# A two-convolution residual block with row transforms: a second PSUM bank for the outer products, the outer sums moved to the end, an opening on TensorE, and a searched assignment of engines

## Chip, cores, metric

One core of one Trainium2 chip. The metric is the device time of one execution in microseconds (us); a kernel's time is the median of its runs. The run of 569.85 us of the kernel before is 1.6% above that kernel's fastest, so it counts as slow and is left out of the ratio below (it is still in the median of 564.35 us; without it the median is 563.33). The profiled span is about 2 us shorter than the time.

## The reference

```python
B, C, HW, E = 2, 512, 64, 1152            # bf16 inputs
def gn(z, gamma, beta): ...               # 4 groups of 128 channels, mean and variance over group and image
def conv3(z, w): ...                      # 3x3, padding 1, 512 -> 512 channels
h = conv3(silu(gn(x, g1, be1)), w1)
h = h + (silu(t_emb) @ w_emb).reshape(B, C, 1, 1)
h = conv3(silu(gn(h, g2, be2)), w2)
return x + h
```

## The kernel before

The 3x3 convolution is computed with transforms over the rows: four output rows come from six products. Planes 0 to 3 ("inner") are sums and differences of input rows, planes 4 and 5 ("outer") serve only the first and the last of the four output rows. VectorE makes the planes ("row sums"), TensorE (PE) multiplies, ScalarE takes the products out of PSUM, and VectorE adds them up to rows. The inner products of chunks 1 to 7 are transformed once more over the columns, which gives B and A matmuls of 256 columns; the others have 512.

The work is cut in 8 chunks (layer, image, half) of four *units* (128 output channels each). Chunks 0 to 3 are layer 1. While the units of chunk c are multiplied, VectorE makes the planes of chunk c+1. The counts of convolution matmuls are 288 in chunk 0, 320 in each of chunks 1 to 3 and 352 in each of 4 to 7, 2656 in all.

The kernel records every operation with its reads and writes and an assumed duration. When the program is built, a list scheduler in the kernel decides the order of each engine's operations. A different assumed duration, or one changed operation, can thus reorder everything.

The end of a unit of layer 2, with cuts marked:

```python
def evac_o(s, bank):                     # outer product -> OO[s - 4], by ScalarE
    act(A(OO[s - 4], [[1, 512]]), Ps(bank, 0, [[1, 512]]), ...)
# ... in unit(c, k), layer 2; `next_pair` cycles through banks 0-1, 2-3, 4-5:
run([(6, 4, plain_mms)]);  evac_o(4, 6)
run([(p1, 0, B_mms), (p1 + 1, 2, B_mms)]);  evac_b(0, p1)
run([(6, 5, plain_mms)]);  evac_o(5, 6)                   # bank 6 again
# ... B of planes 1 and 3, s_ops: BT -> SD
run([(p3, 0, A_mms), (p3 + 1, 2, A_mms)]);  evac_pair(0, p3)     # -> M0, M2
run([(p4, 1, A_mms), (p4 + 1, 3, A_mms)]);  evac_pair(1, p4)     # -> M1, M3
TT(M(0, 4), M(0, 4), A(SD, [[512, 4], [1, 512]]), ALU.add)
TT(two(SD, 512), M(0, 2), M(2, 2), ALU.add)               # s
TT(M(0, 2), M(0, 2), M(2, 2), ALU.subtract)               # d
scal(..., M(2), M(1), -8.0); scal(..., M(3), M(1), -2.0)  # engines by SENG[l]
scal(..., A(SD + 1024, ...), A(SD + 512, ...), 4.0)
tt(M2 and S1, M2 and S1, two(OO[1], OO[0] - OO[1]), ALU.add)     # the outer sum
tt(yr(0),  MB broadcast, M2 and M3, ALU.add)              # rows 0, 1 of the output
tt(yr(16), SD broadcast, S2 and S1, ALU.add)              # rows 2, 3
```

`MB` (M0 to M3), `SD` (S0 to S2) and `BT` exist once. ScalarE may write them for the next unit only when VectorE has read them for this one. Nearly all buffers are stretches of one SBUF array, `ar`.

The small matmuls of the group statistics (`gn_chain`) write two columns of bank 7. The first layer's weights are prepared in chunk 0 by `prep_w1`: a load, two scalings by ScalarE, three or four sums by VectorE.

Of the kernel before, what the change touches and what calls it, by code (L numbers as in the profile page):

```python
# [21 lines left out]
class Op:  # L22
    __slots__ = ("i", "eng", "cost", "lat", "fn", "preds", "succs", "name", "pri", "start", "hold")


class Plan:
# [3 lines left out]
    ENG = ("PE", "DVE", "ACT", "POOL", "DMA", "SW")  # L30
    LAT = {"PE": 0.12, "DVE": 0.1, "ACT": 0.15, "POOL": 0.15, "DMA": 2.0, "SW": 2.6}
# [14 lines left out]
    def op(self, eng, cost, fn, r=(), w=(), name="", chain=False, lat=None, after=()):  # L46
# [3 lines left out]
        o.hold = 0.0  # L50
        deps = set(after)
# [33 lines left out]
    def edge_lat(self, a, b):  # L85
        if a.eng == b.eng:
            return a.lat if a.eng in ("DMA", "SW", "DVE", "POOL") else (0.0 if a.eng == "PE" else a.lat)
        return a.lat

    def _run(self, pri, back):  # L90
# [11 lines left out]
        while done < n:  # L102
# [6 lines left out]
            win = bt + 0.03  # L109
# [76 lines left out]
KAP = (1.0 / 6.0, 1.0 / 24.0, 1.0 / 6.0, 1.0 / 24.0)  # L186

SZ = {}
# [3 lines left out]
def kernel(  # L192
# [15 lines left out]
    UREG, UM = [], 10240  # L208
# [3 lines left out]
    VB = [o, o + 16512 + 14496]  # L212
    Z = o + 16512
    o += 33024 + 14496
    AB = [o, o + AF]
    o += 2 * AF
    WB = o
    o += KF + 1
# [8 lines left out]
    W2O = [Z + 3840, Z + 5376]  # L227
    X0 = Z + 6912
# [3 lines left out]
    O0 = [Z + 11552, Z + 12576]  # L232
# [9 lines left out]
    NF = 480  # L242
# [93 lines left out]
    def dma(out, in_, r, w, nbytes, name="", sw=False, acc=False):  # L336
        rate = 0.14 if (sw and acc) else 0.28
        kw = {"accum_op": ALU.add, "max_dma_last_dim": 2080} if acc else {}
        eng = nc.gpsimd if sw else nc.sync
        pl.op("DMA" if not sw else "SW", nbytes / rate * 1e-6 if nbytes > 30000 else 0.1,  # L340
              lambda: eng.dma_start(out=out, in_=in_, **kw), regs(*r), regs(*w), name)  # L341
# [5 lines left out]
    def mm(lst, name="", chain=True):  # L347
        rr, ww, cost = [], [], 0.0
        for out, lhsT, rhs, st, sp in lst:
            rr += [lhsT, rhs]  # L350
            ww.append(out)
            cost += max(0.06, rhs.n / 2290.0)

        def fn():
            for out, lhsT, rhs, st, sp in lst:
                nc.tensor.matmul(out.ap, lhsT=lhsT.ap, rhs=rhs.ap, start=st, stop=sp, skip_group_check=True)  # L356
        pl.op("PE", cost, fn, regs(*rr), regs(*ww), name, chain=chain)
# [14 lines left out]
    WARM = Fc(2)  # L372
    NEGH = Fc(1)
# [23 lines left out]
    SB = 7  # L397

    def gn_chain(layer, b, ct, mes, name):
# [6 lines left out]
        mm(lst, name, chain=False)  # L406
# [37 lines left out]
    def row_w(w0, w2z, mid, o_um, name):  # L444
# [9 lines left out]
        tt(A(o_um, [[384, 2], [512, 3], [1, 128]]), p3, m, ALU.add, name)  # L454
        tt(A(o_um + 256, [[-128, 2], [512, 3], [1, 128]]), p3, m, ALU.subtract, name)
# [67 lines left out]
    def mode(c):  # L523
        return "N" if c == 0 else ("0" if c < 4 else "1")
# [19 lines left out]
    def load_a(c, ct, resident=None):  # L544
        l, b, ch = chunks[c]
        ab = AB[acnt[0] % 2]
        acnt[0] += 1
        acur[(c, ct)] = (ab, resident)
        nm = f"a{c}{ct}"
        if resident is not None:  # L550
            return
# [15 lines left out]
    def silu(c, ct):  # L567
        l, b, ch = chunks[c]
        ab, res = acur[(c, ct)]
        r0 = RW if ch == 0 else 0  # L570
        dims = [[RW, 33], [33, 2], [1, 32]]
        src = ab if res is None else res
        act(A(ab + r0, dims), A(src + r0, dims, BF16 if l == 0 else None), ACT.Silu,
            scale=F(scol(l, b, ct)), bias=F(ncol(l, b, ct)), name=f"silu{c}{ct}")

    def rows(c, ct, keng="ACT", seng="DVE"):
        ab, _ = acur[(c, ct)]
        nm = f"row{c}{ct}"
        scal(keng, A(WB, [[1, KF]]), A(ab, [[1, KF]]), 4.0, f"k{c}{ct}")
        S, D = ALU.subtract, ALU.add  # L580
        two = lambda base, r0, r1: A(base + r0 * RW, [[(r1 - r0) * RW, 2], [1, PL]])
        tt(two(WB, 9, 17), two(WB, 9, 17), two(ab, 1, 26), S, nm)
        tt(two(WB, 0, 25), two(WB, 0, 25), two(ab, 9, 17), S, nm)
        s4, s5 = vplane(c, ct, 4), vplane(c, ct, 5)
        tt(A(s4, [[s5 - s4, 2], [1, PL]]), two(WB, 0, 25), two(WB, 9, 17), S, nm)
        tt(two(WB, 0, 17), two(ab, 1, 25), two(ab, 9, 17), S, nm)
        t2b = A(WB + 17 * RW, [[1, PL]])
        scal(seng, t2b, t2b, 2.0, nm)
        Q, SS = two(WB, 9, 0), two(WB, 25, 17)
# [7 lines left out]
        for k, op in ((0, D), (2, S)):  # L597
            tt(A(o[k], [[o[k + 1] - o[k], 2], [1, PL]]), Q, SS, op, nm)
        if md == "N":
            return  # L600
# [3 lines left out]
        for kind, (i, j, op) in enumerate(((32, 33, S), (1, 0, S), (33, 0, S), (33, 0, D))):  # L604
# [48 lines left out]
    def unit(c, k, order=None, banks=None):  # L653
# [7 lines left out]
        if md == "1":  # L661
            BT, SD = BT1, SD1
            OO = [UREG[2 * (u % 2)] + 9728, UREG[2 * (u % 2) + 1] + 9728]
        else:
            BT, SD = BT0, SD0
            OO = [O0[u % 2], O0[u % 2] + 512]
        if l == 0 and ch == 0:
            SSUM[(b, k)] = (Fc(12), Fc(2))
        acc = lambda i: None
        if l == 0:  # L670
            cs, cq = SSUM[(b, k)]
            acc = lambda i: F(cs + 6 * ch + i)

        def evac_o(s, bank):
            act(A(OO[s - 4], [[1, 512]]), Ps(bank, 0, [[1, 512]]), ACT.Identity if l == 0 else ACT.Copy,
                scale=(0.25, 1.0)[s - 4], acc=acc(s), name=nm + f"o{s}")

        def evac_m(s, bank, i):
            act(M(s), Ps(bank, 0, [[1, 512]]), ACT.Identity if l == 0 else ACT.Copy, scale=KAP[s], acc=i, name=nm + f"m{s}")
# [4 lines left out]
        def evac_b(s, bank):  # L684
            i = (s // 2) if md == "0" else s
# [7 lines left out]
        def run(steps):  # L693
            for bank, s, fn in steps:
                for ct in range(CT):
                    mm(fn(bank, c, k, ct, s), nm + f"{fn.__name__[0]}{s}")

        TT = tt
        nf = {"N": 0, "0": 2, "1": 4}[md]

        def s_ops():
            g = lambda q: A(BT + q * 256, [[512, nf], [32, 8], [1, 32]])
            TT(A(SD, [[512, nf], [64, 8], [1, 32]]), g(0), g(1), ALU.add, nm + "S")
            TT(A(SD + 32, [[512, nf], [64, 8], [1, 32]]), g(0), g(1), ALU.subtract, nm + "S")

        if order == "ct":
            return
        if md == "N":
            p1, p2 = (banks or (next_pair(), next_pair()))
            run([(6, 4, plain_mms)])  # L710
            evac_o(4, 6)
            run([(p1, 0, plain_mms), (p1 + 1, 2, plain_mms)])
            evac_m(0, p1, acc(1))
            evac_m(2, p1 + 1, None)
            run([(6, 5, plain_mms)])
            evac_o(5, 6)
            run([(p2, 1, plain_mms), (p2 + 1, 3, plain_mms)])
            evac_m(1, p2, acc(3))
            evac_m(3, p2 + 1, acc(2))
        elif md == "0":  # L720
# [3 lines left out]
            run([(p1, 0, B_mms), (p1 + 1, 2, B_mms)])  # L724
            evac_b(0, p1)
            s_ops()
            run([(6, 5, plain_mms)])
            evac_o(5, 6)
            run([(p2, 0, A_mms), (p2 + 1, 2, A_mms)])
            evac_m(0, p2, acc(1))  # L730
            evac_m(2, p2 + 1, None)
            TT(M(0, 2, 1024), M(0, 2, 1024), A(SD, [[512, 2], [1, 512]]), ALU.add, nm + "A")
# [3 lines left out]
        else:  # L736
# [5 lines left out]
            run([(6, 5, plain_mms)])  # L742
            evac_o(5, 6)
# [7 lines left out]
            TT(M(0, 4), M(0, 4), A(SD, [[512, 4], [1, 512]]), ALU.add, nm + "A")  # L751

        two = lambda off, st: A(off, [[st, 2], [1, 512]])
        TT(two(SD, 512), M(0, 2), M(2, 2), ALU.add, nm + "s")
        TT(M(0, 2), M(0, 2), M(2, 2), ALU.subtract, nm + "d")
        se = SENG[l]
        scal(se[0], M(2), M(1), -8.0, nm + "8")
        scal(se[1], M(3), M(1), -2.0, nm + "2")
        scal(se[2], A(SD + 1024, [[1, 512]]), A(SD + 512, [[1, 512]]), 4.0, nm + "4")

        tt(two(MB + 1024, SD + 512 - MB - 1024), two(MB + 1024, SD + 512 - MB - 1024), two(OO[1], OO[0] - OO[1]),
           ALU.add, nm + "O")
        yr = lambda r0: A(ys + r0 * RW, [[RW, 16], [33, 2], [1, 32]])
        tt(yr(0), A(MB, [[0, 2], [64, 8], [1, 64]]) if False else A(MB, [[0, 2], [1, 512]]),
           A(MB + 1024, [[512, 2], [1, 512]]), ALU.add, nm + "y")
        tt(yr(16), A(SD, [[0, 2], [1, 512]]), A(SD + 1024, [[-512, 2], [1, 512]]), ALU.add, nm + "y")
        yv = A(ys, [[1, YF]])
        if l == 0:
            dma(h_scr[b, k, ch], yv.ap, [yv], [K("h", b, k, ch)], P * YF * 2, nm + "st")
            act(A8(JNK, YF), yv, ACT.Square, scale=float(HW) ** -0.5, acc=F(cq + ch), name=nm + "sq")  # L770
            if ch == 1:
                gn2(b, k)
        else:
            dma(out[b, k, ch], yv.ap, [yv, K("o", b, k, ch)], [K("o", b, k, ch)], P * YF * 2, nm + "out", sw=True, acc=True)
        ucnt[0] += 1

    SENG = {0: ("DVE", "DVE", "DVE"), 1: ("ACT", "ACT", "ACT")}

    def gn2(b, k):
        cs, cq = SSUM[(b, k)]  # L780
        m0, me, wj, ws = Fc(2), Fc(2), Fc(12), Fc(1)
# [32 lines left out]
    def stats0(ct):  # L814
# [3 lines left out]
        x0 = A(XB0[ct] + RW, [[1, YF]], BF16)  # L818
        x1 = A(XB1[ct], [[1, YF]], BF16)
        bk = 4 + (ct % 2)  # L820
        lst = []
        for h, base in enumerate((XB0[ct] + RW, XB1[ct])):
            for i in range(5):
                lst.append((Ps(bk, 0, [[1, 416]]), cone, A(base + i * 416, [[1, 416]], BF16),
                            h == 0 and i == 0, h == 1 and i == 4))
        mm(lst, nm, chain=False)
        junk = A(MB + (ct % 2) * 512, [[1, 416]], BF16)
        act(junk, Ps(bk, 0, [[1, 416]]), ACT.Identity, scale=1.0 / (P * HW), acc=F(me), name=nm)
        act(A8(JNK, YF), x0, ACT.Square, scale=float(HW) ** -0.5, acc=F(me + 1), name=nm)
        bg = ct % 4  # L830
        lst = []
        for i in range(17):
# [178 lines left out]
```

## Time and profile before

| | before |
|---|---|
| time, median (lowest to highest) | 564.35 us (560.69 to 569.85), 4 runs |
| profiled span, mean granted clock | 558.7 us, 0.943 |
| matmuls of 512 / 256 columns | 1248 / 1408 |
| VectorE: 16-bit sums of 1024 elements | 304, 0.692 us each as recorded |

From the page of the kernel before: the busy times with their shares of the span, and busy tenths in 40 slices with the clock that PE was granted.

```profile
## 1 busy us (share of the span) xinstructions
PE 479.6 (86%) x2853; PEld 280.0 (50%) x2853; DVE 446.8 (80%) x943; ACT 404.7 (72%) x627; POOL 36.7 (7%) x62
...
PE   5649996999798889898997789987999896989990
...
DVE  1898898896599897987677999898899888974543
ACT  6998787699798968584565878565889776655551
...
PEclk9959997999999989999997879998999997999995
```

No engine is busy all the time. From its waits (who waited for whom, total us, times, longest):

```profile
ACT ar L328 <- PE psum L356: 72.3, 67, 5.5
DVE ar L305 <- ACT ar L328: 55.3, 45, 2.9
ACT ar L328 <- DVE ar L305: 46.0, 35, 5.4
...
PE psum L356 <- DVE ar L305: 38.1, 16, 5.4
PE psum L356 <- ACT ar L328: 15.0, 7, 4.9
```

ScalarE waits for PE, VectorE for ScalarE, ScalarE for VectorE, and PE for both: a ring. L328 is the line of all ScalarE operations, L305 of all VectorE sums, L356 of all matmuls. Four stretches of PE's timeline (start, length, what; in brackets the idle time before it and what ended it):

```profile
30.74 1.44 PE L356 MATMUL psum<-ar 128*128 128x512 f16 x3 [5.09 <-DVE ar L305]
37.58 43.96 PE L356 MATMUL psum<-ar 128*128 128x512 f16 x186 [5.40 <-DVE ar L305]
...
204.18 30.43 PE L356 MATMUL psum<-ar 128*128 128x512 f16 x160 [2.45 <-ACT ar L328]
...
469.39 30.30 PE L356 MATMUL psum<-ar 128*128 128x512 f16 x188 [4.89 <-ACT ar L328]
```

The first two are the opening, which waits for row sums. The other two are the first matmul of the second outer block, which waits for bank 6. Three windows of layer 2 (length, then busy us and count of PE, weight loads, VectorE, ScalarE, POOL; clock; DMA share; GB/s):

```profile
380.00:400.00 20.00, 18.79 (x118) 12.02 (x117) 17.11 (x42) 15.45 (x19) 3.57 (x4) 0.93 0.51 100
400.00:420.00 20.00, 18.84 (x146) 14.17 (x146) 19.57 (x43) 15.92 (x15) 4.14 (x5) 1.00 0.66 159
420.00:440.00 20.00, 17.31 (x119) 11.28 (x118) 18.09 (x34) 15.77 (x16) 1.46 (x4) 1.00 0.46 119
```

### The profile page before, as it was taken

Reading aid. Unit: us, or ns where it says so; the run is one execution under the profiler, and the core shown is the slowest. Engines: PE = TensorE matmul, PEld = TensorE weight load, DVE = VectorE, ACT = ScalarE, POOL = GpSimd, SP = SyncE. Lnnn points to the kernel's source line nnn. Section 1 sums busy time; section 2 is a strip of 40 time slices with the busy share of each in tenths; the row PEclk is TensorE's granted clock in tenths of the full one; section 3 lists DMA queues with packets and bytes.
Section 4 is the critical chain, followed back from the end, with each engine's and each line's share of the span. In section 5 each row is a group of like instructions: output and inputs, shape, how many; then the busy total and the mean of one; then the engine's idle time right before and its main releaser. Section 6 shows DMA issues by size and latency. Waiting matters only on the chain.

```text
span 558.7 us, 8160 instructions
## 1 busy us (share of the span) xinstructions
PE 479.6 (86%) x2853; PEld 280.0 (50%) x2853; DVE 446.8 (80%) x943; ACT 404.7 (72%) x627; POOL 36.7 (7%) x62
## 2 busy tenths in 40 slices
PE   5649996999798889898997789987999896989990
PEld 3414442455354445454553356655666563767760
DVE  1898898896599897987677999898899888974543
ACT  6998787699798968584565878565889776655551
POOL 2100000000000000000000000101210000001000
PEclk9959997999999989999997879998999997999995
DMA  8576556766645345333445543564556564454432
GB/s 338 213 226 211 158 164 189 240 230 193 223 166 181 127 131 193 125 134 114 175 175 182 181 144 101 136 160 104 118 153 136 135 152 88 98 121 93 65 54 38
DMA packets 37465, 86.11 MB, mean 154 GB/s; under 512 B 6064, under 2 KB 15792, under 8 KB 37424
## 3 DMA queue, kind: packets, MB, share of 16 engines
q1 hardware_dynamic: 32784, 77.06, 42.3%
q0 software_dynamic: 4352, 8.52, 10.4%
q8 instruction: 22, 0.36, 0.3%
q14 instruction: 19, 0.16, 0.1%
q10 hardware_dynamic: 288, 0.01, 0.0%
HBM read 62.25 MB, written 31.85 MB: 168 GB/s over the span
## 4 chain that ended last, share of the span: by engine, by line
issue 19%; DVE 15%; PE 10%; ACT 5%; DMA 3%; POOL 2%; POOLq 0%; DVEq 0%; SPq 0%; ACTq 0%
DVE ar L305 14%; PE psum L356 10%; ACT ar L328 5%; DMA ar<-h_scr 2%; POOL out_dram L341 2%; DMA ar<-in_w_dram 1%; DVE ar L309 0%; POOL fs L415 0%; POOLq L1006 0%; DVEq L305 0%; DVE fs L801 0%; DVE fs L422 0%; DVE fs L409 0%; DVE fs L420 0%; DVE fs L408 0%
## 5 line engine op out<-in xcount | busy, mean ns | idle before, releaser
L356 PE MATMUL psum<-ar 128*128 128x512 f16 (+2 forms) x2732 | 462.0, 330 | 51.6 <-DVE ar L305 38.1
L305 DVE TENSOR_TENSOR ar<-ar 128x1024 f16<-128x1024 f16 (+6 forms) x688 | 417.1, 653 | 81.4 <-ACT ar L328 55.3
L356 PEld LDWEIGHTS <-ar 128*128 128x128 f16 (+1 forms) x2724 | 266.4, 99 | 243.2 <-issue 71.2
L328 ACT ACTIVATE ar<-psum 128x512 f16<-128x512 f32 (+2 forms) x220 | 155.3, 714 | 96.0 <-PE psum L356 72.3
L328 ACT ACTIVATE ar<-ar 128x384 bf16<-128x384 bf16 (+6 forms) x208 | 188.2, 936 | 34.3 <-DVE ar L305 24.4
L328 ACT ACTIVATE ar<-ar,fs 128x2112 f16<-128x2112 bf16 (+1 forms) x32 | 68.7, 2145 | 9.3 <-DVE fs L422 3.8
L341 POOL DMA_DIRECT2D out_dram<-ar x16 | 19.4, 1215 | 151.9 <-DVE ar L305 151.4
L415 POOL TENSOR_TENSOR fs<-fs 128x1 f32<-128x1 f32 x16 | 12.3, 772 | 222.0 <-DVE fs L412 222.0
L309 DVE TENSOR_SCALAR ar<-ar 128x512 f16<-128x512 f16 (+2 forms) x84 | 23.9, 312 | 0.9 <-ACT ar L328 0.8
L328 ACT ACTIVATION_READ_ACCUMULATOR ar<-psum 128x1 f32 x96 | 19.0, 198 | 0.0
L328 ACT ACTIVATION_READ_ACCUMULATOR ar<-ar 128x1 f32 x68 | 13.1, 193 | 0.0
L356 PE MATMUL psum<-ar,ones_bf 128*128 128x416 bf16 x40 | 9.1, 383 | 4.4 <-DMA ar<-in_x_dram 4.4
L345 POOL MEMSET ar<- 128x65 f16 (+2 forms) x22 | 3.7, 210 | 139.8 <-ACT ar L328 93.5
L356 PE MATMUL psum<-fs,ones_neg 128*128 128x1 f32 (+1 forms) x72 | 9.6, 237 | 3.4 <-DVE ar L841 1.7
L356 PEld LDWEIGHTS psum<-fs,ones_neg 128*128 128x128 f32 x72 | 10.0, 190 | 5.0 <-DVE ar L841 1.9
L356 PEld LDWEIGHTS <-ones_bf 128*128 128x128 bf16 x40 | 4.4, 114 | 7.8 <-issue 4.7
L356 PE MATMUL psum<-ar,s_sb 128*2 128x512 bf16 x9 | 3.5, 542 | 4.8 <-DVE fs L408 4.8
L420 DVE TENSOR_TENSOR fs<-fs 128x1 f32<-128x1 f32 x16 | 2.5, 155 | 3.6 <-POOL fs L415 3.5
L841 DVE SCALAR_TENSOR_TENSOR ar<-psum,ident 128x128 bf16<-128x128 f32 x4 | 1.1, 287 | 5.1 <-PE psum L356 5.1
L408 DVE COPY fs<-psum 128x2 f32<-128x2 f32 x16 | 2.5, 155 | 3.2 <-PE psum L356 2.8
L356 PEld LDWEIGHTS <-s_sb 128*2 128x2 bf16 x9 | 0.8, 101 | 7.0 <-issue 6.9
L422 DVE SCALAR_TENSOR_TENSOR fs<-fs 128x1 f32<-128x1 f32 x16 | 3.4, 213 | 0.1
(35 smaller groups left out, 23.1 us busy)
## 6 DMA issues: line engine op xcount, KB each, us to landing
ar<-in_w_dram SPq DMA_DIRECT2D x32, 384.0 KB, 3.6
ar<-in_x_dram SPq DMA_DIRECT2D x16, 552.5 KB, 4.6
out_dram<-in_x_dram SPq DMA_DIRECT2D x16, 520.0 KB, 5.0
h_scr<-ar SPq DMA_DIRECT2D x16, 520.0 KB, 3.7
ar<-h_scr SPq DMA_DIRECT2D x16, 520.0 KB, 3.5
out_dram<-ar POOLq DMA_DIRECT2D x16, 520.0 KB, 6.0
u_scr<-ar SPq DMA_DIRECT2D x16, 384.0 KB, 3.3
ar<-u_scr SPq DMA_DIRECT2D x4, 1536.0 KB, 7.5
```

The source lines that it names most:

```text
L305: pl.op("DVE", 0.075 + 0.000521 * out.n, lambda: nc.vector.tensor_tensor(out=out.ap, in0=a.ap, in1=b.ap, op=op), regs(a, b), regs(out), name)
L309: pl.op("DVE", cost or 0.075 + 0.00026 * out.n, lambda: nc.vector.tensor_scalar(out=out.ap, in0=a.ap, scalar1=s, scalar2=None, op0=ALU.mul ...
L328: lambda: nc.scalar.activation(out=out.ap, in_=a.ap, func=func, scale=sc, **kw), regs(*rr), regs(*ww), name)
L341: lambda: eng.dma_start(out=out, in_=in_, **kw), regs(*r), regs(*w), name)
L345: pl.op("POOL" if eng == "gpsimd" else "DVE", 0.08 + 0.0005 * out.n, lambda: e.memset(out.ap, v), (), regs(out), name)
L356: nc.tensor.matmul(out.ap, lhsT=lhsT.ap, rhs=rhs.ap, start=st, stop=sp, skip_group_check=True)
L408: pl.op("DVE", 0.16, lambda: nc.vector.tensor_copy(out=F(tot, 2).ap, in_=ps.ap), regs(ps), regs(F(tot, 2)), name)
L415: pl.op("POOL", 0.25, lambda: nc.gpsimd.tensor_tensor(out=F(rs).ap, in0=F(nv).ap, in1=F(NEGH).ap, op=ALU.pow), regs(F(nv)), regs(F(rs)), name)
L420: pl.op("DVE", 0.1, lambda: nc.vector.tensor_mul(out=F(s).ap, in0=F(rs).ap, in1=F(g).ap), regs(F(rs)), regs(F(s)), name)
L422: pl.op("DVE", 0.1, lambda: nc.vector.scalar_tensor_tensor(out=F(nb).ap, in0=F(tot).ap, scalar=F(s).ap, in1=F(g + CT).ap, op0=ALU.mult, op ...
L841: pl.op("DVE", 0.3, lambda: nc.vector.scalar_tensor_tensor(out=j2.ap, in0=g.ap, scalar=1.0 / HW, in1=ident[:], op0=ALU.mult, op1=ALU.mult, ...
```

## The change

The intent, as the change puts it: two outer banks, outer sums by DMA or VectorE, opening statistics on TensorE, first unit block-major, engine choices searched. The core of the diff, with cuts:

```diff
-            run([(6, 5, plain_mms)])
-            evac_o(5, 6)
+            run([(7, 5, plain_mms)])
+            evac_o(5, 7)
...                                    # the outer sum moves behind the last two additions
-        tt(two(MB + 1024, SD + 512 - MB - 1024), two(MB + 1024, ...), two(OO[1], OO[0] - OO[1]), ALU.add, nm + "O")
         tt(yr(0), A(MB, [[0, 2], [1, 512]]), A(MB + 1024, [[512, 2], [1, 512]]), AD, nm + "y")
         tt(yr(16), A(SD, [[0, 2], [1, 512]]), A(SD + 1024, [[-512, 2], [1, 512]]), AD, nm + "y")
+        yo = A(ys, [[24 * RW, 2], [1, PL]])
+        oo = A(OO[1], [[OO[0] - OO[1], 2], [1, PL]])
+        if CFG["oacc"][l] and not last: dma(yo.ap, oo.ap, ..., sw=True, acc=True)
+        else: tt(yo, yo, oo, AD, nm + "O")
...                                    # statistics recorded behind the next unit, not before it
-                gn2(b, k)
+                later.append(lambda: gn2(b, k))
...
+CFG = {'k0': (D_, D_, D_, D_), 't0': D_,
+    'k': (D_, D_, A_, D_, A_, A_, D_, A_), 't': (D_, D_, A_, D_, A_, A_, A_, D_),
+    's': ((A_, A_, A_), (D_, D_, D_), (D_, A_, A_), (D_, D_, D_), (A_, A_, A_), (A_, A_, D_), (A_, A_, A_), (D_, A_, D_)),
+    'st1': (1, 0, 1, 1), 'oacc': (0, 0), 'np': 1, 'wpe': (1, 0, 0, 0), 'vacc': (1, 0, 0, 1, 0, 0, 0, 0)}
...                                    # opening: outer products of units 0 to 2, channel block by block
+        for j in range(3):
+            mm(plain_mms(2 * j, 0, j, ct, 4), "o")
+            mm(plain_mms(2 * j + 1, 0, j, ct, 5), "o")
...                                    # row sums: the outer planes get their last addend at the end,
+                dma(d.ap, t.ap, ..., sw=True, acc=True)      # by DMA in chunk 3 (vacc),
+                tt(v45, v45, t0, AD, nm)                     # else by VectorE
...                                    # planner: latencies, look-ahead, 2.5 us of slack for small matmuls
-    LAT = {"PE": 0.12, "DVE": 0.1, "ACT": 0.15, "POOL": 0.15, "DMA": 2.0, "SW": 2.6}
+    WIN = {"DMA": 0.6}
+    LAT = {"PE": 0.12, "DVE": 0.12, "ACT": 0.15, "POOL": 0.15, "DMA": 2.1}
```

With `oacc` at (0, 0), all outer sums stay on VectorE.

## The prediction

> **What bounds it now.** The busy table shows PE 480, VectorE 447 and ScalarE 405 of 558.7 us: no single engine. The trace holds 1248 matmuls of 512 columns and 1408 of 256 for the convolutions; at the spacing of unbroken stretches (about 0.215 and 0.11 us) that is an estimated 420 us of full-clock PE. The gaps between PE's matmuls show where it stands still: (a) the opening: convolution matmuls run steadily only from 37.6 us, after waits of 5.1 and 5.4 us for VectorE, and then start at half speed (0.43 us apart; the clock row shows 0.7 in that slice, which agrees with "TensorE: Matmul & The Clock Gate", section "What's actually happening": an idle array is throttled to half); (b) six waits at the first matmul of the second outer block, on ScalarE, because both outer blocks use bank 6: 0.4, 1.3, 2.5, 2.7, 1.7, 4.9, together 13.4 us; (c) about 25 us on VectorE's row sums and evictions' sums. In the windows view VectorE is 85 to 97% busy from 20 to 500 us except 260-300; by the counts of its operations it needs about 15.4 us per unit in chunks 1-2, 17 in chunk 3 and 13.3 in chunks 4-6, where PE needs 13.7 and 11.9. So VectorE sets the pace up to chunk 7, PE after (12.4 us per unit, from the spacing of the last output stores), then 15 us of tail. VectorE itself loses 55 us waiting for ScalarE and 14 for reloads.
>
> **What the change does.** From the instruction order of both kernels, costed with the trace's means:
> - VectorE: +12 scalings of 2145 (0.72 each, +8.6), +8 statistics (about +5.4), -16 scalings of 520 (-4.8), -8 of 512 (-2.3), -4 sums given to DMA (-2.8), -1 weight preparation (-1.7): net about +2, so 447 becomes about 449. Outer sums by DMA are switched off for the outputs; only four plane sums use it.
> - ScalarE: -12 scalings of 2145 (1.99 each, -24), -12 statistics pairs (-12), +24 small scalings (+15): 405 becomes about 384.
> - PE: some 24 more statistics matmuls and 12 for one weight block, under 4 us, all in the opening's shadow.
> - Bank 7 for the second outer block: removes (b), 13.4 us at PE; I count half, since VectorE limits those stages.
> - Opening: 72 outer matmuls of units 0-2 (about 15.5 us of PE) run while later channel blocks are still prepared, keeping the clock up; the first unit runs block-major. Chunk 0 then ends by VectorE, not PE: I count 8 us.
> - The 2 us ScalarE scaling leaves the path between SiLU and row sums in chunks 1, 3 and 6, and evictions queue less: of the 55 us I count 6 to 10.
>
> **Sum.** About 7 + 8 + 8 = 23 us off. Nothing lowers VectorE's total, so much larger gains are unlikely: VectorE's own floor (its work from 13.5 us on plus chunk 7 and tail) is about 496 us. Predicted 540 us (-4%), range 524 to 555; chances 0.84 faster by over 2%, 0.13 within, 0.03 slower.
>
> **What would show it.** VectorE busy 440-455, ScalarE 375-392, PE's waits on ScalarE at the second outer block gone, PE wait total down from 64 to under 40 us, steady convolution matmuls before 25 us, mean clock above 0.95, first output store before 335 us (347 now); VectorE's wait for ScalarE under 45 us.
>
> **What would make it wrong.** Waits removed at PE return as VectorE waits; the searched choices fit the planner's durations and not the chip's; putting x1's square on ScalarE delays the first SiLU (11.6 us now); the four DMA sums (landing several us) delay planes in chunk 3; or the search removed VectorE's stalls far better than I allow (below 524).

## The result

The changed kernel takes 526.18 us (524.82 to 526.81, 4 runs) against 564.35 us. The ratio is 0.934, with a 95% interval of 0.929 to 0.939. Ratios here are the mean time of one kernel's fast runs over that of the other's in the same rounds, so not quite the ratio of the medians. From the page of the changed kernel:

```profile
## 1 busy us (share of the span) xinstructions
PE 473.8 (91%) x2889; PEld 281.2 (54%) x2889; DVE 445.7 (85%) x932; ACT 383.9 (73%) x614; POOL 44.1 (8%) x75
...
PE   6999986664999999999995999999999999999990
...
DVE  1799757588799999999999999999999999986443
ACT  4896838588999986686987678597866878665440
...
PEclk9999989785999999999998999999999999999995
```

Its waits (the line numbers shifted: L341 is ScalarE, L318 the VectorE sums, L369 the matmuls, L421 the copy of the statistics out of PSUM):

```profile
ACT ar L341 <- DVE ar L318: 68.0, 58, 4.6
...
DVE ar L318 <- ACT ar L341: 31.6, 24, 3.9
ACT ar L341 <- PE psum L369: 29.8, 34, 1.7
...
PE psum L369 <- DVE ar L318: 21.8, 8, 6.7
...
PE psum L369 <- DVE fs L421: 8.1, 5, 5.3
```

ScalarE's wait for PE fell from 72.3 to 29.8 us and VectorE's for ScalarE from 55.3 to 31.6. PE no longer waits for ScalarE. From PE's timeline:

```profile
114.39 4.00 PE L369 MATMUL psum<-ar 128*128 128x512 f16 x9 [4.30 <-DVE ar L318]
125.10 4.00 PE L369 MATMUL psum<-ar 128*128 128x512 f16 x15 [6.71 <-DVE ar L318]
...
284.27 14.59 PE L369 MATMUL psum<-ar 128*128 128x512 f16 x70 [5.31 <-DVE fs L421]
...
326.69 182.38 PE L369 MATMUL psum<-ar 128*128 128x256 f16 x1300
```

The first two lines wait for the row sums of chunk 1, the third for the statistics in bank 7 (see e10). The last line is 1300 matmuls in 182.38 us without a stop: nearly all of layer 2. The same windows as before:

```profile
380.00:400.00 20.00, 20.00 (x148) 14.13 (x147) 19.97 (x35) 13.47 (x17) 1.35 (x2) 1.00 0.65 168
400.00:420.00 20.00, 20.00 (x146) 13.98 (x145) 19.90 (x32) 14.91 (x16) 2.56 (x3) 1.00 0.54 125
420.00:440.00 20.00, 20.00 (x143) 13.68 (x142) 19.83 (x34) 17.59 (x18) 2.70 (x4) 1.00 0.64 159
```

PE and VectorE are both busy for 19.8 us or more of every 20. To see where the time came from, I counted the convolution matmuls in each trace and took the end of the last one of each chunk (these ends are modelled by the profile). End of chunk 0, then the length of each later chunk, in us:

| kernel | time | end of 0 | 1 | 2 | 3 | 4 | 5 | 6 | 7 |
|---|---|---|---|---|---|---|---|---|---|
| before | 564.35 | 113.9 | 65.9 | 67.7 | 66.4 | 60.6 | 57.9 | 60.3 | 51.3 |
| changed | 526.18 | 110.1 | 75.6 | 59.9 | 64.6 | 50.3 | 49.5 | 49.5 | 49.5 |

The spans differ by 35.7 us. Layer 1 gives 3.6 us of it (313.8 less 310.2 at its end), layer 2 gives 31.1 and the tail 1.0. Chunk 0 ends 3.8 us earlier, but chunk 1 takes 9.7 us more, so at its end the changed kernel is behind.

### The profile page after: what moved, and what is told of

Read it like the earlier page. It is cut to its first block, busy times and chain, and to the rows that moved or that the text cites. A ratio compares the mean times of both kernels' runs of the same rounds, so it can differ in the third digit from the quotient of the medians.

```text
span 523.0 us, 8270 instructions
## 1 busy us (share of the span) xinstructions
PE 473.8 (91%) x2889; PEld 281.2 (54%) x2889; DVE 445.7 (85%) x932; ACT 383.9 (73%) x614; POOL 44.1 (8%) x75
## 4 chain that ended last, share of the span: by engine, by line
issue 21%; DVE 20%; PE 6%; POOL 2%; ACT 2%; POOLq 0%; DVEq 0%; ACTq 0%
DVE ar L318 19%; PE psum L369 6%; POOL out_dram L354 2%; ACT ar L341 2%; DVE ar L322 1%; POOLq L1121 0%; DVE fs L846 0%; DVE fs L422 0%; DVE fs L435 0%; POOL ar L358 0%; DVE fs L433 0%; DVE fs L421 0%; DVE fs L841 0%; POOLq L354 0%; DVE fs L425 0%
## 5 line engine op out<-in xcount | busy, mean ns | idle before, releaser
L369 PE MATMUL psum<-ar 128*128 128x256 f16 (+2 forms) x2737 | 456.1, 327 | 30.1 <-DVE ar L318 21.8
L318 DVE TENSOR_TENSOR ar<-ar 128x1040 f16<-128x1040 f16 (+6 forms) x681 | 412.2, 654 | 48.6 <-ACT ar L341 31.6
L369 PEld LDWEIGHTS <-ar 128*128 128x128 f16 (+1 forms) x2729 | 264.4, 98 | 216.0 <-issue 31.5
L341 ACT ACTIVATE ar<-ar 128x512 f16<-128x512 f16 (+7 forms) x206 | 169.7, 852 | 62.0 <-DVE ar L318 47.9
L341 ACT ACTIVATE ar<-psum 128x512 f16<-128x512 f32 (+2 forms) x221 | 154.7, 716 | 55.6 <-PE psum L369 29.8
L341 ACT ACTIVATE ar<-ar,fs 128x2112 f16<-128x2112 bf16 (+1 forms) x32 | 68.5, 2144 | 7.4 <-DMA ar<-h_scr 2.6
L354 POOL DMA_DIRECT2D out_dram<-ar x16 | 19.3, 1206 | 126.8 <-DVE ar L318 105.6
L322 DVE TENSOR_SCALAR ar<-ar 128x512 f16<-128x512 f16 (+2 forms) x72 | 26.0, 385 | 1.6 <-ACT ar L341 1.6
L341 ACT ACTIVATION_READ_ACCUMULATOR ar<-psum 128x1 f32 x96 | 19.4, 202 | 0.0
L369 PE MATMUL psum<-ar,ones_bf 128*128 128x260 bf16 x64 | 10.1, 317 | 4.4 <-DMA ar<-in_x_dram 4.4
L358 POOL MEMSET ar<- 128x65 f16 (+4 forms) x27 | 4.6, 212 | 110.9 <-DVE ar L318 38.2
L369 PEld LDWEIGHTS psum<-fs,ones_neg 128*128 128x128 f32 x72 | 10.3, 206 | 2.5 <-DVE fs L958 1.6
L341 ACT ACTIVATION_READ_ACCUMULATOR ar<-ar 128x1 f32 x56 | 10.7, 191 | 0.0
L369 PE MATMUL psum<-fs,ones_neg 128*128 128x1 f32 (+1 forms) x72 | 10.0, 247 | 0.7 <-DVE fs L958 0.7
L369 PEld LDWEIGHTS <-ones_bf 128*128 128x128 bf16 x64 | 6.9, 112 | 6.2 <-issue 3.1
L354 POOL DMA_DIRECT2D ar<-ar x4 | 3.7, 922 | 73.6 <-ACT ar L341 52.2
L421 DVE COPY fs<-psum 128x2 f32<-128x2 f32 x16 | 2.5, 156 | 6.8 <-PE psum L369 6.8
L969 DVE BATCH_NORM_STATS2 fs<-ar 128x6 f32<-128x512 bf16 x8 | 5.4, 686 | 0.0
```

The costliest lines, as they stand in the source:

```text
L318: pl.op("DVE", 0.075 + 0.000521 * out.n, lambda: nc.vector.tensor_tensor(out=out.ap, in0=a.ap, in1=b.ap, op=op), regs(a, b), regs(out), name)
L322: pl.op("DVE", cost or 0.075 + 0.00026 * out.n, lambda: nc.vector.tensor_scalar(out=out.ap, in0=a.ap, scalar1=s, scalar2=None, op0=ALU.mul ...
L341: lambda: nc.scalar.activation(out=out.ap, in_=a.ap, func=func, scale=sc, **kw), regs(*rr), regs(*ww), name)
L354: lambda: eng.dma_start(out=out, in_=in_, **kw), regs(*r), regs(*w), name, lat=3.2 if sw else None)
L358: pl.op("POOL" if eng == "gpsimd" else "DVE", 0.08 + 0.0005 * out.n, lambda: e.memset(out.ap, v), (), regs(out), name)
L369: nc.tensor.matmul(out.ap, lhsT=lhsT.ap, rhs=rhs.ap, start=st, stop=sp, skip_group_check=True)
```

## Experiments

Twelve kernels ran, all correct, each timed in 3 rounds against the kernel before. The table has the same columns, from each run's profile.

| run | time | ratio to before | end of 0 | 1 | 2 | 3 | 4 | 5 | 6 | 7 |
|---|---|---|---|---|---|---|---|---|---|---|
| e1_one_bank | 541.94 | 0.961 | 108.5 | 68.4 | 68.4 | 62.2 | 58.4 | 53.7 | 57.4 | 49.5 |
| e2_old_planner | 527.82 | 0.937 | 112.0 | 76.7 | 59.8 | 63.1 | 50.3 | 49.5 | 49.9 | 50.6 |
| e3_old_order | 559.31 | 0.992 | 109.2 | 79.0 | 60.0 | 68.7 | 50.6 | 59.8 | 54.9 | 59.6 |
| e4_old_choices | 541.43 | 0.959 | 128.3 | 77.7 | 62.2 | 58.9 | 51.0 | 49.5 | 49.5 | 49.5 |
| e5_old_rows | 528.75 | 0.938 | 110.5 | 82.8 | 58.0 | 59.2 | 50.3 | 50.5 | 51.6 | 50.8 |
| e6_old_outer | 558.06 | 0.990 | 111.4 | 81.8 | 63.1 | 80.0 | 50.3 | 56.4 | 49.5 | 50.2 |
| e7_null | 533.45 | 0.947 | 107.9 | 78.9 | 62.2 | 68.5 | 50.3 | 50.1 | 50.1 | 50.7 |
| e8_pre_pinned | 525.77 | 0.933 | 107.8 | 74.9 | 61.5 | 67.0 | 50.3 | 49.5 | 50.3 | 49.5 |
| e9_before_outer | 525.87 | 0.931 | 114.3 | 58.9 | 63.2 | 60.0 | 56.8 | 57.7 | 50.6 | 49.6 |
| e10_before_both | 616.26 | 1.090 | 168.4 | 81.4 | 64.1 | 82.8 | 56.2 | 49.6 | 49.6 | 49.6 |
| e11_raw4 | 518.84 | 0.919 | 101.9 | 75.7 | 60.0 | 63.0 | 50.3 | 49.5 | 51.5 | 49.5 |
| e12_hold | 544.65 | 0.968 | 106.2 | 86.3 | 61.8 | 66.3 | 50.3 | 53.5 | 52.8 | 50.4 |

### Undoing one part at a time: e1 to e4

**e1, one bank.** In all modes of the changed kernel:

```diff
-            run([(7, 5, plain_mms)])
-            evac_o(5, 7)
+            run([(6, 5, plain_mms)])
+            evac_o(5, 6)
```

> The changed kernel with both outer blocks in bank 6 again (bank 7 keeps only the small statistics sums). Prediction's theory (the bank is worth about 7 us, since VectorE limits the stages): 533 us, with waits at the second outer block back in layer 2. Bank theory (the stop-free PE run of layer 2, 49.5 us per chunk instead of 58-61, is due to the bank): layer 2 chunks go back to 55 us or more and the time to 545 us or more. If the bank is worth nothing: 526 us.

541.94 us, 15.8 above the changed kernel, and more than all of it in layer 2 (20 us more there, less in chunks 0 to 3): chunks 4 to 6 take 58.4, 53.7 and 57.4 us. The bank theory's 545 was not quite reached, but my 7 us were too few. In PE's timeline of this run, the direct wait for the bank is a small part:

```profile
315.51 52.42 PE L369 MATMUL psum<-ar 128*128 128x512 f16 x352 [5.67 <-DVE ar L318]
369.31 1.49 PE L369 MATMUL psum<-ar 128*128 128x512 f16 x9 [1.38 <-DVE ar L318]
...
425.25 29.88 PE L369 MATMUL psum<-ar 128*128 128x512 f16 x195 [3.64 <-DVE ar L318]
456.47 70.03 PE L369 MATMUL psum<-ar 128*128 128x512 f16 x500 [1.34 <-ACT ar L341]
```

Only the last of these four is a second outer block. The others wait for row sums, so most of the loss shows elsewhere than at the bank. How a late bank comes to delay the row sums was not traced.

**e2, old planner constants.** `LAT`, `WIN`, the DMA rate and the slack as before.

> The changed kernel with the planner constants of before (VectorE latency 0.10, DMA latency 2.0 and rate 0.28, DMA look-ahead 0.03, no slack for the small matmuls). Planner theory: the new order of instructions is what removed the layer 2 waits, time 540 us or more. Rival (the structure does it, the constants only shift the order a little): 526 us plus or minus 4.

527.82 us: the constants are worth 1.6 us or nothing.

**e3, old order of sums.** Row sums in the order of before in chunks 1 to 7, and the outer sum before the last two additions (on M and S, with two stretches of 512 elements in each operand, as before). This gives up the four sums by DMA.

> The changed kernel with the row sums in the order of before for all chunks after the first (outer planes early, no sum by DMA) and the outer sum again before the last two additions, on contiguous operands. Dependence theory (the late outer sum and late plane sum free VectorE from waiting for ScalarE): VectorE's wait for ScalarE rises from 32 us towards 55 and the time by 8 us or more, to 534 us or more. Rival (same operations, same total, so nothing): 526 to 529 us (3 us for the four sums that return from DMA).

559.31 us: nearly the whole gain is gone.

**e4, old engine choices.** `CFG` set to the fixed choices of before.

```diff
-    'k': (D_, D_, A_, D_, A_, A_, D_, A_),
+    'k': (D_, A_, A_, A_, A_, A_, A_, A_),
... # t all VectorE; s VectorE in layer 1, ScalarE in layer 2; st1 all ScalarE; wpe, vacc 0
```

> The changed kernel with the engine choices of before (ScalarE scalings of 2145 in all later chunks, layer 1 small scalings on VectorE, layer 2 on ScalarE, all statistics of the second image on ScalarE, no weight block by TensorE, no sum by DMA). Choices theory: ScalarE is back at about 404 us busy, VectorE waits for it, time 538 us or more. Rival (in layer 2, where 29.5 us of the 35.7 us were won, the choices hardly differ): layer 2 chunks stay at 49 to 51 us, the time rises by at most 8 us, in layer 1.

541.43 us, 15.3 more. Both theories were partly right. ScalarE is back at 403.2 us busy, and yet layer 2 stays at 49.5 to 51 us per chunk. The loss is in chunk 0, which ends at 128.3 instead of 110.1. There, four choices meet: one weight block on TensorE, one set of statistics on VectorE, the small scalings on ScalarE, and the scaling of 2145 for the rows of chunk 1 on VectorE. Which of them counts was not tried.

### Which sum, and how much is luck: e5 to e8

**e5 and e6, the halves of e3.** e5 has the old row sums alone:

```diff
-        rows_a(c, ct, WB[0], CFG["k"][c], False)
-        rows_b(c, ct, WB[0], CFG["t"][c], False, CFG["vacc"][c])
+        rows_a(c, ct, WB[0], CFG["k"][c], True)
+        rows_b(c, ct, WB[0], CFG["t"][c], True)
```

e6 has the old place of the outer sum alone:

```diff
+        tt(tw(MB + 1024, SD + 512 - MB - 1024), tw(MB + 1024, ...), tw(OO[1], OO[0] - OO[1]), AD, nm + "O")
         yr = lambda r0: A(ys + r0 * RW, [[RW, 16], [33, 2], [1, 32]])
...
-        yo = A(ys, [[24 * RW, 2], [1, PL]])
-        ...                                  # and the late sum
```

> Half of e3 (559 us): only the row sums in the order of before for chunks 1 to 7 (no sum by DMA), the outer sum stays last. If the row order made e3's loss: 545 to 560 us with layer 2 stops in chunks 4 to 6, none in 7 (it produces no rows). If the outer sum made it: 526 to 532 us.

> The other half of e3: only the outer sum back before the last two additions. Theory: this sum sits between the evictions and the last two additions that free the single M and S buffers, so ScalarE's next evictions, and with them the PSUM pairs, come free later: 545 to 558 us, stops of PE at the B and A groups in chunks 5 to 7 as in e3. Rival: 526 to 532 us. If both halves cost, each lies near 540.

e5: 528.75 us, which is the four sums that return from DMA or nothing. e6: 558.06 us. So the outer sum's place makes 32 us, with the operands that go with it: one VectorE operation per unit, early on 1024 elements of M and S, late on 1040 of the output rows. In the waits of e6, the ring is back, though this kernel has both outer banks:

```profile
ACT ar L341 <- PE psum L369: 67.8, 64, 3.2
ACT ar L341 <- DVE ar L318: 65.5, 63, 5.5
...
PE psum L369 <- DVE ar L318: 47.6, 19, 9.7
DVE ar L318 <- ACT ar L341: 45.6, 39, 3.4
```

Compare the changed kernel: 29.8, 68.0, 21.8 and 31.6. Its lost time is for the most part in chunks 1, 3 and 5 (6.2, 15.4 and 6.9 us), not in all of them.

The kept traces say more about this sum, which can be picked out by the shape of its operands. In the kernel before, VectorE stood idle for 30.2 us in all directly before its 32 early outer sums, in e3 for 29.7 and in e6 for 19.3. Before the late ones of the changed kernel and of e9 it stood idle for 0.2 us in all. Of the 30.2 us, 16.9 ended with the landing of a load of h or x, which the sum does not read. PE, too, waited for the early sum, which no matmul reads: ten times in the kernel before, 16.7 us in all, and eleven times in e6, 25.5 us, each time starting about 0.05 us after the sum had ended, and each time in an odd chunk. One sum of the kernel before, in VectorE's timeline and in PE's (the sum is the first of the three operations):

```profile
302.02 2.04 DVE L305 TENSOR_TENSOR ar<-ar 128x1024 f16<-128x1024 f16 x3 [3.14 <-DMA ar<-h_scr]
...
302.76 13.07 PE L356 MATMUL psum<-ar 128*128 128x512 f16 x55 [3.87 <-DVE ar L305]
```

So the early sum costs waits that its own reads and writes do not ask for, and this is shown. Why they are there is only inferred. The early sum takes M2 and S1 as one operand, which reaches across all that lies between S and M in `ar`: the planes of the odd chunks, the load buffers and the output rows. It looks as if the waits, which are set when the program is built, treat that operand as touching everything between. The planner lists exact elements and knows of no such waits. An early sum split in two, one for M2 and one for S1, would be the test; it was not run.

**e7, a null change.** `rate = ... else 0.305` for `0.31` in the planner. The traces show the same number of matmuls in another order.

> A change of nothing but the planner's assumed DMA rate, 0.305 for 0.31: the same operations in another order of about the same quality. It shows how much a reshuffled plan alone moves the time. Structure theory: 524 to 531 us. Luck theory (the plan of the change is a searched one, and any other order loses): 535 us or more, as e1, e3 and e4, which would then prove little.

533.45 us: a reshuffled plan alone cost 7.3 us. Both theories get a part. Differences of 7 us between re-planned kernels decide nothing; 15 and 32 us are beyond what this one null showed.

**e8, copies moved with every other order pinned.** After the planner has run, only the start of the 32 copies of x to the output is moved:

```diff
     pl.solve()
+    st = {o.name: o.start for o in pl.ops}
+    for o in pl.ops:
+        if o.name.startswith("pre"):
+            c, k = int(o.name[3]), int(o.name[4])
+            o.start = st[f"u{c - 3}{k}" + ("st" if c < 7 else "out")] + 0.01
```

> The changed kernel with every compute engine's order kept; only the 32 copies of x to the output are moved in the DMA queue from chunks 0 and 1 to chunks 1 to 4. Theory: the copies hold up the loads of weights and x in the first 130 us (VectorE idles 22 us from 60 to 140 us, 11 us of it marked as waiting for loads), so chunk 1 ends 10 us earlier and the time falls to 516 us. Rival: the loads are late for another reason (their buffers come free late): 526 us, unchanged stops.

525.77 us, no change. Chunk 0 ended 2.3 us earlier, and it was given back by chunk 3. My theory that the copies hold up the loads failed.

### Doing parts alone on the kernel before: e9, e10

**e9, the late outer sum alone.**

```diff
-            act(A(OO[s - 4], [[1, 512]]), Ps(bank, 0, [[1, 512]]), ...
+            act(A(OO[s - 4], [[RW, 8], [33, 2], [1, 32]]), Ps(bank, 0, [[1, 512]]), ...
...
-        tt(two(MB + 1024, SD + 512 - MB - 1024), two(MB + 1024, ...), two(OO[1], OO[0] - OO[1]), ALU.add, nm + "O")
...
+        yo = A(ys, [[24 * RW, 2], [1, PL]])
+        tt(yo, yo, A(OO[1], [[OO[0] - OO[1], 2], [1, PL]]), ALU.add, nm + "O")
... # buffers of OO padded to 8 rows of 65, pad columns zeroed
```

> The kernel before with one thing of the change alone: the outer sum moved to the end, onto the output buffer. If the place of the outer sum is the main cause by itself: 540 us or less. If it only works together with the second bank (both outer blocks still share bank 6 here): 552 to 565 us. A reshuffled plan alone moved the time by 7 us (e7), so less than that decides nothing.

525.87 us: the time of the whole change, from one moved addition (and the padded buffers that it needs), with one bank, the old opening, the old choices and the old planner. The gain lies elsewhere than in the changed kernel: 7.0, 4.5 and 6.4 us in chunks 1 to 3, and 15.4 in layer 2. PE still waits at the shared bank, but for less:

```profile
402.79 37.36 PE L356 MATMUL psum<-ar 128*128 128x512 f16 x264 [1.86 <-ACT ar L328]
440.96 70.11 PE L356 MATMUL psum<-ar 128*128 128x512 f16 x500 [0.82 <-ACT ar L328]
```

Both lines are second outer blocks: 1.86 and 0.82 us.

**e10, the late outer sum and the second bank.** e9 and the two lines of e1, the other way round.

> The kernel before with the late outer sum and the second outer bank, nothing else (no opening blocks, old engine choices, old row order, old planner constants). Theory: these two make the stop-free layer 2, so chunks 4 to 6 fall from 58-61 to 49.5-52 us each and the time to 530 to 542 us. Rival (the engine choices or the opening are needed for it): 548 us or more, chunks 4 to 6 at 55 us or more.

616.26 us, 51 slower than before, which neither theory foresaw. PE's timeline:

```profile
87.37 1.01 PE L356 MATMUL psum<-fs,ones_neg 128*128 128x2 f32 x4 [19.38 <-DVE fs L877]
...
123.24 1.02 PE L356 MATMUL psum<-fs,ones_neg 128*128 128x2 f32 x4 [16.67 <-DVE fs L877]
...
154.79 1.01 PE L356 MATMUL psum<-fs,ones_neg 128*128 128x2 f32 x4 [11.55 <-DVE fs L877]
...
216.23 0.98 PE L356 MATMUL psum<-fs,ones_neg 128*128 128x2 f32 x4 [7.13 <-DVE fs L796]
```

The waits of 19.38, 16.67 and 11.55 us stand before the small statistics matmuls (four of 2 columns or fewer). These write bank 7. In the kernel before they are recorded ahead of the unit, so the unit's second outer block, once it is in bank 7, has to come after them in PE's order. They in turn wait for a sum of partial statistics that VectorE makes late. The change records the statistics behind the next unit (`later`): that is what lets it use bank 7. The Trainium skill's "PSUM — Partial Sum Buffer", section "PSUM bank collisions raise a hardware error", asks to guard PSUM by bank, not by address. This kernel's planner does so (it lists PSUM by its 8 banks), and thus two columns can hold up a whole block. The changed kernel agrees on a smaller scale: its 5.31 us wait at 284.27 is a second outer block that waits for the copy of two columns out of bank 7. Layer 2 of e10, from chunk 5 on, runs at 49.6 us per chunk: there, the late sum and the second bank are enough, without the new choices.

### The loss in chunk 0, and holding the buffers: e11, e12

**e11, four buffers for the raw taps.**

```diff
+    RAWX = [o, o + 1152]
+    o += 2304
...
-        rb = RAW[rawc[0] % 2]
+        rb = (RAW + RAWX)[rawc[0] % 4]
```

> The changed kernel with four buffers instead of two for the raw middle taps of the first layer's weights. Theory (e8 failed: the loads of chunk 0 are not late because of the copies, but because they wait for one of two buffers that VectorE frees): VectorE's and ScalarE's waits for weight loads from 40 to 140 us fall from about 14 to under 5 us, conv matmul 288 ends before 104 us (110 now), the time falls to 514 to 521 us. Rival (loads were not the limit of that stage; the sums of the first unit are): 524 to 530 us.

518.84 us, the fastest kernel. Its interval against before (0.914 to 0.924) lies below that of the changed kernel (0.929 to 0.939), but the 7.3 us that it gained are no more than what the null of e7 cost, so the size of the gain is not secure. VectorE's waits from 30 to 178 us, first of the changed kernel, then of e11:

```profile
DVE ar L318 <- ACT ar L341: 8.4, 9, 2.8
DVE ar L318 <- DMA ar<-in_w_dram: 7.4, 3, 2.9
DVE ar L318 <- DMA ar<-in_x_dram: 3.7, 2, 2.3
```

```profile
DVE ar L320 <- ACT ar L343: 10.9, 10, 2.7
...
DVE ar L320 <- DMA ar<-in_x_dram: 1.4, 1, 1.4
```

The 7.4 us of waiting for weights are gone and chunk 0 ends 8.2 us earlier, at 101.9 us; in the other re-planned variants of the changed kernel that kept its engine choices it ended between 106.2 and 112.0. So the loads were late because their buffers came free late, not because of the copies. Together with ScalarE's (4.4 us in the changed kernel and 4.0 here, from 40 to 140 us), they fell from 11.8 to 4.0 us, as expected, but on VectorE alone. The Trainium skill's "Perfetto Trace Analysis", section "Optimization Strategy", names too few buffers as a possible cause of repeated bubbles; this run agrees. Chunk 1 did not shorten (75.7 us); it remains 17 us longer than in e9, and that was not explained.

**e12, the buffers held.** A tiny copy behind the late outer sum reads six elements of M and S:

```diff
             tt(yo, yo, oo, AD, nm + "O")
+        held = A(SD, [[MB - SD, 2], [512, 3], [1, 1]])
+        pl.op("DVE", 0.1, lambda: nc.vector.tensor_copy(out=<6 floats of scratch>, in_=held.ap), regs(held, yo), ...)
```

> The changed kernel plus one tiny VectorE copy per unit, right after the late outer sum, that reads six elements of the M and S buffers into a scratch: it costs about 0.1 us of VectorE per unit (3 us in all) and keeps M and S from being overwritten until the outer sum is done, as the early sum of before did by its place. Hold theory (the late sum pays because M and S, which exist once, are free one addition of 0.7 us and one wait earlier, so that ScalarE's evictions and with them PSUM are not held up): 545 us or more, near e6's 558. Rival (the early sum costs for another reason, as its wait for the outer evictions or the order of the plan): 526 to 536 us (3 us for the copies, up to 7 for a reshuffled plan).

544.65 us, 18.5 above the changed kernel and at the edge of the hold theory's "545 or more". VectorE's busy time rose by 6.4 us (452.1 less 445.7), twice what I allowed. What is left, about 12 us, is more than the 7.3 us of the null, but not by much. But the run is no clean test of the hold theory, because the operand of the copy also reaches from S to M. VectorE stood idle for 14.1 us in all directly before the 32 copies, and 9.2 us of that ended with the landing of a DMA. With the 6.2 us of the copies themselves this is as much as the whole loss. ScalarE also waited for the copies, ten times and 19.6 us in all, before it took products out of PSUM, which is what the hold theory says. So how much of the 32 us is holding M and S, and how much is waiting for buffers that the sum does not use, stays open.

## Why the prediction was right, and where it was not

The time of 526.18 us lies in the predicted range of 524 to 555, near its lower end; the loss predicted was 24 us and 38 came. The direction and most of the signs held:

- VectorE busy 445.7 us (predicted 440 to 455), ScalarE 383.9 (375 to 392). The costing of added and removed operations was right.
- PE's idle time before matmuls fell from 64 to about 35 us (under 40 predicted), the clock is 0.957, the first output store is issued at 332.5 us (before 335).
- PE's wait for ScalarE at the second outer block is gone.
- Steady convolution matmuls came at 26.95 us, not before 25. The Trainium skill's "TensorE: Matmul & The Clock Gate", section "What's actually happening", says that an idle array is throttled to half. Both traces agree: the kernel before started after its waits with matmuls 0.43 us apart, against 0.23 later, at a mean clock of 0.70 from 20 to 40 us; the changed one has 1.00 there.

That the three terms, 23 us in all, put the time inside the range is luck: none of them was right in both place and size.

- "Opening ... I count 8 us": 3.8 us at the end of chunk 0, and a deficit of 6.0 us at the end of chunk 1. The opening keeps PE busy, but VectorE lost time to late weight loads (e11).
- "I count half, since VectorE limits those stages" (7 us for the bank): undoing it costs 15.8 us (e1), with an uncertainty of the order of e7's 7.3. Added to the kernel before with the late sum alone it costs 90 us (e10 less e9). The bank has no worth of its own: it depends on when the statistics are recorded. The prediction did not see that bank 7 was in use.
- "Evictions queue less: ... I count 6 to 10": the choices are worth 15.3 us (e4), but all of it by the end of chunk 0. I had placed it at the rows of "chunks 1, 3 and 6", which are made during chunks 0, 2 and 5; chunk 5 shows nothing, and chunk 2 only 2.3 us (62.2 less 59.9).

Two steps failed.

**The outer sum was read as neutral.** The prediction says that outer sums by DMA are switched off, and costs nothing for their new place. That place alone gives the whole gain on the kernel before (e9, 38 us) and, undone, takes 32 of 38 us from the changed kernel (e6). The early sum was not neutral where it stood: VectorE idled 30.2 us directly before the 32 early sums and 0.2 us before the late ones. Since e9, e1, e4 and e6 sum to far more than the gain, the parts are not additive: each relieves the same ring of waits.

**VectorE was held to be the limit of layer 2 at 13.3 us per unit.** The measured pace is 12.4 us (49.5 us for four units), with PE and VectorE both full. PE's need was put too low, at 11.9 us: at the start-to-start times of unbroken stretches in both traces, about 0.226 us for 512 columns and 0.109 for 256, a unit takes PE 24 x 0.226 + 64 x 0.109 = 12.4 us, so layer 2 now runs at PE's own pace. VectorE's need was put too high, since I had multiplied counts by recorded durations. These overlap, as the kernel before shows in one line of VectorE's timeline:

```profile
338.75 4.96 DVE L305 TENSOR_TENSOR ar<-ar 128x1024 f16<-128x1024 f16 x8
```

Eight sums recorded at a mean of 0.692 us take 4.96 us together, 0.62 each; each overlaps the next by about 0.08 us (8 x 0.692 less 4.96, over seven). With that, the estimate for VectorE would have been 13.3 x 0.62 / 0.69 = 12.0 us per unit, a little below PE's 12.4. Layer 2 of the kernel before, at 14.5 to 15.2 us per unit, then had over 2 us per unit of pure waiting to win, in place of the 1 to 2 that I saw.

## What to carry to other kernels

Where buffers exist once and three engines pass them around, ask of each operation not only what it costs but what it holds and what it is made to wait for: an addition moved behind the last readers of a shared buffer cost nothing and was worth as much as a large rewrite. Look in the trace for waits that an operation's reads and writes do not explain, above all where one operand reaches across other buffers. Take an engine's pace from the start-to-start times of a full stretch, not from recorded durations times counts. Before giving a spare PSUM bank a second user, look at when its first user's matmuls are placed in PE's order, and where a scheduler orders the program, run one null change first to know the noise of a reshuffle.

## What the Trainium skill lacked or had wrong

- "PSUM — Partial Sum Buffer" has the rule to guard by bank, but nothing on what a shared bank can cost: four small matmuls in a bank shared with a large block held PE up for 19.38 us (e10).
- None of the pages used here gives the noise of a reordered program: the same operations in another order of similar quality took 7.3 us more of 526 (e7).
- None of the pages used here speaks of waits on buffers that an operation does not touch: VectorE idled 16.9 us before early outer sums of the kernel before until loads had landed that these sums do not read.
